# Small e-row moves on ScalarE's queue with two row tiles, and a new order of loads and matrix units between the two passes

## The chip, the cores and the metric

The kernel runs on one core of one Trainium2 chip. Its time is the device time of that core in microseconds (us). Five engines work beside each other: TensorE (PE; its weight loads are listed as PEld), VectorE (DVE), ScalarE (ACT), GpSimd (POOL) and SyncE (SP). SyncE and ScalarE can issue transfers that hardware turns into descriptors, GpSimd issues transfers through software; all of them are carried out by the same 16 DMA engines.

## The reference

One token of width 640 goes through an adaptive-LayerNorm block: attention over a cache (32 heads, 8192 keys, head width 192), then a gated mixer and an MLP (640 to 1536 to 640). The function returns the block's output and the gradients for nine inputs, among them both caches, which are by far the largest tensors (100.7 MB each, and as much again for each gradient).

```
q      = (h @ wq) per head
scores = q . k * Dh**-0.5 ;  p = softmax(scores)
o      = p @ v ;  attn = o @ wo
x1     = x + ga * attn
out    = x1 + gb * B(layernorm(x1) * (1 + cb) + sb)
# gradients wanted: x, k_cache, v_cache, wq, wo, w3, w4, c, w_mod
dV = p^T do          dP = do . V
dS = p * (dP - sum)  dK = dS^T q
```

With a single query, every product of the attention is a matrix with a vector, so the work is reading K once and V twice (once in each pass) and writing dK and dV.

## The kernel before, in words

A head's 8192 keys lie as 128 partitions by 64 rows; a half is 32 rows (1536 KB in bf16), a quarter 16. The work has two passes with a middle between them.

**First pass.** A loop over heads `i` from 0 to 30 holds three heads at once: it computes the scores of head `i`, scales V of head `i - 1` by its exponentials, and finishes head `i - 2`. Scores are a VectorE product (`dot_mul`, L307), a folding sum (L312) and sums of identity matmuls on TensorE (L318). The scaled V tiles (`vs`, four quarters for each head, in a pool of three buffers) feed matmuls with K that build M = K^T (e V) for the head (`m_units`, L391 and L396), which the gradient of q needs later. `m_units` gives four pieces for a quarter, of eight matmuls each: two for the first 128 columns of K and two for the remaining 64. `mp_out` and `m_add` copy M out of PSUM and add its two parts. `E_all` keeps the exponentials of all heads. SyncE issues all loads, in the order in which they stand: K and V halves, wq and w_mod chunks, wo for each pair of heads (`load_wo`, 480 KB, L210), and near the end rows of w4 (L616 to L618).

**Middle.** From L620 head 31 is scored in quarters (`score_mul`, `score_tree`), its exponentials and those of head 30 are multiplied with the unscaled V (`o_rows`, L414), the last pair's output goes through wo (`pair_ao`), and x1 and the two LayerNorms follow as chains of very small VectorE steps with matmuls for the means (`mean_mm`, `mean_sum`). Between them stand the four units `mz[0]` to `mz[3]` of head 29's last quarter, and the row sums `dg_part(n)` (L526), which multiply n of the twelve rows of w4 with a broadcast vector; they use w4 from `w4b`, from `w4x` (a buffer of the `vs` pool) and from `KY` (a K buffer). Then u = LN(x1) @ w3, its gradient and the vectors that the second pass needs (`dao`, `do_r`, `cpr`) are computed.

**Second pass.** It goes over 64 steps `s`, a half of a head each. For each step VectorE multiplies V with `do` (`mul_q`, L1030), TensorE sums (`tree_q`, L1039) to dP, VectorE forms dS (L1334) and dK (`dk_part`, L1055). dV is an outer product: `dv_groups` takes the e rows of the step, which lie across the partitions 0, 32, 64 and 96 in a tile `er_b`, multiplies them with `do` in groups (L1050), and ScalarE copies each group out of PSUM (L1051) into the buffer that GpSimd stores (`store`, L1282). There are eight such groups to a step.

**E rows.** `e_rows(t)` (L337 to L342) transposes the exponentials of a pair of heads on TensorE into PSUM, and ScalarE copies them into a row tile `er_t`. `load_er(s)` (L848 to L854) then moves 32 rows of 256 bytes of it into `er_b[s % 2]`, 8 KB in all, by a DMA from SBUF to SBUF. The first two moves stand just ahead of the second pass (L1013); the later ones are issued in `dv_gen`, where step `s` has done its eighth group: there `load_er(s + 2)` refills the buffer that step `s` has just read. A new row tile is made every fourth step. In between, side jobs (`g_do`, `g_dwo`, `g_chunk` and others) are spread over the steps' slots.

**Order.** From L529 on `tc.manual_schedule(engines=ORDER)` holds for the rest of the kernel: the instructions of TensorE, VectorE, ScalarE and SyncE, with their DMAs, keep the order in which they are written. GpSimd is not in `ORDER`; the framework places its instructions.

```
ORDER = {mybir.EngineType.PE, mybir.EngineType.DVE, mybir.EngineType.Activation, mybir.EngineType.SP}
```

Of the kernel before, what the change touches and what calls it, by code (L numbers as in the profile page):

```python
# [8 lines left out]
FP32 = mybir.dt.float32  # L9
BF16 = mybir.dt.bfloat16  # L10
# [10 lines left out]
def kernel(  # L21
# [26 lines left out]
    nc = tc.nc  # L48
    P = 128
    D = A_x.shape[-1]  # L50
    _, HQ, S, DH = A_k_cache.shape
# [4 lines left out]
    JH = J // 2  # L56
    JQ = J // 4
    TS = 16
    ND = D // P
# [6 lines left out]
    VW = DH + 4  # L66
# [6 lines left out]
    V_, A_, T_ = nc.vector, nc.scalar, nc.tensor  # L73
# [10 lines left out]

    dram = ctx.enter_context(tc.tile_pool(name="dram", bufs=1, space=bass.MemoryType.DRAM))
    ORDER = {mybir.EngineType.PE, mybir.EngineType.DVE, mybir.EngineType.Activation, mybir.EngineType.SP}
    erp = ctx.enter_context(tc.tile_pool(name="erp", bufs=1))

    A_.preload_act_table_set("natural_log_exp_and_others")
    ident_bf = const.tile([P, P], BF16, name="ident_bf")  # L90
# [26 lines left out]
    def mean_mm(src, n):  # L117
        ps = psS.tile([P, 16], FP32, name="mean_ps", tag="s")
        T_.matmul(ps[:, 0:n], lhsT=onesD, rhs=src, start=True, stop=True)
        return ps  # L120
# [86 lines left out]
    def load_wo(t):  # L207

        w = wst.tile([P, 3, D], BF16, name="wo_st", tag="wo")
        nc.sync.dma_start(out=w, in_=wo_v[t])  # L210
        return w
# [41 lines left out]
    n0, r0 = layernorm(x_c, "ln0")  # L253
# [39 lines left out]
    def flat(kb):  # L293
        return kb.rearrange("p j d -> p (j d)")
# [6 lines left out]
    def load_v(h, t, v):  # L301
        nc.sync.dma_start(out=v, in_=V_hd[h][:, t * JH : (t + 1) * JH, :])
        return v
# [24 lines left out]
    H1 = HQ - 1  # L328
    TL = NT - 1
    KX, KY, KC, KD, KE = (KB[(2 * HQ + k) % NKB] for k in (-4, -5, -3, -2, -1))  # L330
# [13 lines left out]
    with tc.tile_pool(name="vs", bufs=3) as vsp, tc.tile_pool(name="ft", bufs=2) as ft, \  # L344
# [40 lines left out]
        def m_units(q, kb, vs, mp, last=3):  # L385
            j0 = (q % 2) * JQ
            z = q == last

            def main(lo, hi):
                for k in range(lo, hi):  # L390
                    T_.matmul(mp[:, 0:MW], lhsT=kb[:, j0 + k, 0:P], rhs=vs[:, k, 0:MW], start=(q == 0 and k == 0), stop=(z and k == JQ - 1), skip_group_check=True)  # L391

            def rest(lo, hi):
                for k in range(lo, hi):
                    p0 = 64 * (k % 2)
                    T_.matmul(mp[p0 : p0 + 64, MO : MO + MW], lhsT=kb[:, j0 + k, P:DH], rhs=vs[:, k, 0:MW], start=False, stop=(z and k >= JQ - 2), skip_group_check=True)  # L396

            return [lambda: main(0, JQ // 2), lambda: main(JQ // 2, JQ), lambda: rest(0, JQ // 2), lambda: rest(JQ // 2, JQ)]
# [11 lines left out]
        def o_rows(h, v2, op, lo, hi):  # L410

            for j in range(lo, hi):
                p0 = 32 * (j % 4)
                T_.matmul(op[p0 : p0 + 32, 0:DH], lhsT=E_all[:, h, j : j + 1].to_broadcast([P, 32]), rhs=v2[j // JH][:, j % JH, :], start=(j < 4), stop=(j >= J - 4), skip_group_check=True)  # L414
# [11 lines left out]
        def mp_out(h, mp):  # L426
            mt = ft.tile([P, MW], FP32, name="mt", bufs=1)
            if h == H1 - 2:
                A_.copy(out=mt[64:128, :], in_=mp[64:128, MO : MO + MW])
            A_.copy(out=M1[:, h, :], in_=mp[:, 0:MW])  # L430
            if h != H1 - 2:
                A_.copy(out=mt[64:128, :], in_=mp[64:128, MO : MO + MW])
            return mt
# [7 lines left out]
        def m_add(h, mp, mt):  # L441
            t, b = divmod(h, 2)
            V_.tensor_tensor(out=M2[64 * b : 64 * b + 64, t, :], in0=mp[0:64, MO : MO + MW], in1=mt[64:128, :], op=ALU.add)
# [28 lines left out]
        X, os_, wo_l = {0: {"k": [load_k(0, 0), load_k(0, 1)], "v": [load_v(0, 0, VB[0])]}}, {}, {}  # L472
# [3 lines left out]
        w4v = B_w4.rearrange("(a p) r -> p a r", p=P)  # L476
# [26 lines left out]
        def w4r(a):  # L503
            if a < 3:
                return w4b[:, a * D : (a + 1) * D]
            if a == 3:
                return w4b[:, 5 * D : 6 * D]
            c0 = (a - 8) * D if a >= 8 else JQ * DH + (a - 4) * D
            return flat(KY)[:, c0 : c0 + D]

        def load_w4(lo, dst, n=4):
            nc.sync.dma_start(out=dst[:, 0 : n * D].rearrange("p (a r) -> p a r", r=D), in_=w4v[:, lo : lo + n, :])

        def w4_at(a):
            if a == 4:
                return w4b[:, 3 * D : 4 * D]
            return w4x[:, (a - 5) * D : (a - 4) * D] if 5 <= a < 8 else w4r(a)

        def dg_junk(a):
            if a == 3:  # L520
                return w4x[:, 3 * D : 4 * D]
            return w4b[:, 3 * D : 4 * D] if a >= 8 else w4_at(a)

        def dg_part(n):
            for a in dgs[:n]:
                V_.tensor_tensor_reduce(out=dg_junk(a), in0=w4_at(a), in1=dbo_bc, scale=1.0, scalar=0.0, op0=ALU.mult, op1=ALU.add, accum_out=d_g[:, a : a + 1])  # L526
            del dgs[:n]

        ctx.enter_context(tc.manual_schedule(engines=ORDER))  # L529
        if True:  # L530
            for i in range(H1):
# [3 lines left out]
                z = X.pop(i - 2) if i > 1 else None  # L535
# [28 lines left out]
                if z is not None:  # L564
                    mt = m_out(i - 2, z["mp"], z["op"], os_)
# [22 lines left out]
                if y is not None:  # L588
                    vs = scale_v(2, y["v"][1], E4, Ef)
# [15 lines left out]
                for f in late:  # L605
                    f()
                nx["v"].append(load_v(i + 1, 0, VB[(2 * i + 2) % NVB]))
                if i % 2 == 1:
                    wo_l[(i + 1) // 2] = load_wo((i + 1) // 2)
                early(i, "end")  # L610
                if i == H1 - 3:

                    w4b = wst.tile([P, ND * CW], BF16, name="w4b", tag="w", bufs=1)
                    dbo_bc, du_bc = w4b[:, 4 * D : 5 * D], w4b[:, 0:F]
                    bcast_cols(dbo, ND, dbo_bc, A_.copy)
                    nc.sync.dma_start(out=w4b[:, 0 : 3 * D].rearrange("p (a r) -> p a r", a=3), in_=w4v[:, 0:3, :])  # L616
                    nc.sync.dma_start(out=w4b[:, 5 * D : 6 * D], in_=w4v[:, 3, :])
                    nc.sync.dma_start(out=w4b[:, 3 * D : 4 * D], in_=w4v[:, 4, :])  # L618
                if i > H1 - 3:
                    dg_part(1)  # L620
            assert mb == NMB and wch is None
# [1 line left out]

            x, y, z = X[H1], X[H1 - 1], X[H1 - 2]
            x["v"].append(load_v(H1, 1, VX))
            mz = m_units(3, z["k"][1], z["vs"], z["mp"])
            x["S"] = ft.tile([P, J], FP32, name="S_h")
            qh = q_at(H1)
# [42 lines left out]
            op_y = psO.tile([P, 256], FP32, name="op")  # L671
            o_rows(H1 - 1, vy, op_y, 0, JH)
            w3d = B_w3.rearrange("(i p) n -> p i n", p=P)
            w4x = vsp.tile([P, JQ, VW], BF16, name="vs").rearrange("p j d -> p (j d)")
            load_w4(5, w4x, 3)
            load_w4(8, flat(KY))
            score_tree(1, d0)
            score_mul(1, 0)
            score_tree(0, d1)
# [6 lines left out]
            w3p = flat(pp.tile([P, JH, DH], BF16, name="w3p", tag="prod"))  # L686
            nc.sync.dma_start(out=w3p[:, 0 : 4 * F].rearrange("p (i n) -> p i n", i=4), in_=w3d[:, 0:4, :])
            nc.sync.dma_start(out=w4b[:, 0:F], in_=w3d[:, 4, :])
            w3v = [w3p[:, k * F : (k + 1) * F] for k in range(4)] + [w4b[:, 0:F]]
            dot_sum(d1, x["S"][:, JH:J])  # L690
            mx = row_max(x["S"])
# [11 lines left out]
            po_x = psr([P, 8], FP32, "po_x")  # L703
            op_x = psO.tile([P, 256], FP32, name="op")
            o_rows(H1, x["v"], op_x, 0, JH)
            o_rows(H1, x["v"], op_x, JH, J)
            es_x = e_sum(H1)
            os_out(1, op_x, es_x)
            dg_part(3)
            for b in range(2):  # L710
                T_.matmul(po_x[64 * b : 64 * b + 64, 3:4], lhsT=onesD[:, 0:64], rhs=os2[:, 2 * DH + b : 2 * DH + b + 1], start=True, stop=True, skip_group_check=True)
            T_.matmul(po_x[:, 4:6], lhsT=onesD, rhs=os2[:, 2 * DH : 2 * DH + 2], start=True, stop=True, skip_group_check=True)
# [8 lines left out]
            V_.tensor_tensor(out=xP, in0=ga, in1=aoP, op=ALU.mult)  # L721
            V_.tensor_tensor(out=xP, in0=xP, in1=x_c, op=ALU.add)
            ps_ao = pair_ao(o2, wo_l[TL], psB, "b")
            mz[1]()
            aoN = col(ND, "aoN")
            V_.reduce_sum(out=aoN, in_=ps_ao, axis=AX.X)
            V_.tensor_tensor(out=x1, in0=ga, in1=aoN, op=ALU.mult)
            V_.tensor_tensor(out=x1, in0=x1, in1=xP, op=ALU.add)
            A_.copy(out=AO[:, :, 2 * TL : 2 * TL + 2], in_=ps_ao)
            ps = mean_mm(x1, ND)  # L730
            mz[2]()
            dg_part(1)
            m = mean_sum(ps, 1, "ln_m")
            xc = col(ND, "ln_xc1")
            V_.tensor_scalar(out=xc, in0=x1, scalar1=m[:, 0:1], scalar2=None, op0=ALU.subtract)
# [1 line left out]
            V_.tensor_tensor(out=pr[:, 0:ND], in0=xc, in1=xc, op=ALU.mult)  # L737
            V_.tensor_tensor(out=pr[:, ND : 2 * ND], in0=xc, in1=a1, op=ALU.mult)
            ps = mean_mm(pr, 2 * ND)
            mz[3]()  # L740
            dg_part(1)
            vt = col(2, "ln_vt")
            V_.reduce_sum(out=vt, in_=ps[:, 0 : 2 * ND].rearrange("p (a b) -> p a b", b=ND), axis=AX.X)
# [7 lines left out]
            ps = mean_mm(pr, 2 * ND)  # L751
            xc2 = col(ND, "ln_xc2")
            V_.scalar_tensor_tensor(out=xc2, in0=zz, scalar=r1[:, 0:1], in1=sS, op0=ALU.mult, op1=ALU.add)
            mt = mp_out(H1 - 2, z["mp"])
            er_t = [e_rows(TL, psB, "b")]
            m_add(H1 - 2, z["mp"], mt)
            ab = mean_sum(ps, 2, "ln_ab")
            v2 = col(1, "ln_v2")
            V_.tensor_scalar(out=v2, in0=ab[:, 0:1], scalar1=r1[:, 0:1], scalar2=ab[:, 1:2], op0=ALU.mult, op1=ALU.add)
# [4 lines left out]
    bst = ctx.enter_context(tc.tile_pool(name="bst", bufs=1))  # L764
# [83 lines left out]
    def load_er(s):  # L848

        er = er_b[s % 2]  # L850
        h, t = ht(s)
        r0 = (h % 2) * J + t * JH
        nc.gpsimd.dma_start(out=er[0:P:32, :, :], in_=er_t[0][r0 : r0 + JH, :])  # L853
        return er  # L854

    def ht(s):
# [149 lines left out]
    nc.sync.dma_start(out=dao_bc, in_=dao_d.to_broadcast([P, D]))  # L1006
    V_.tensor_scalar(out=dx1, in0=e4, scalar1=vv[:, 0:1], scalar2=-1.0, op0=ALU.add, op1=ALU.mult)
    V_.tensor_tensor(out=dao, in0=dx1, in1=ga, op=ALU.mult)
    cpp, cp1 = bst.tile([P, DH], FP32, name="dq_junk")[:, 0 : HQ * ND].rearrange("p (h k) -> p h k", k=ND), bst.tile([P, HQ], FP32, name="cp1")
    V_.tensor_tensor(out=cpp, in0=AO.rearrange("p k h -> p h k"), in1=dao[:, None, :].to_broadcast([P, HQ, ND]), op=ALU.mult)  # L1010
    V_.reduce_sum(out=cp1, in_=cpp, axis=AX.X)
    V_.memset(er_b[1], 0.0)
# [400 lines left out]
```

## Time and profile before

| | |
|---|---|
| median of 4 runs | 1409.81 us (1403.95 to 1410.89) |
| the profiled execution: its own time | 1403.95 us |
| its span, first to last instruction | 1402.2 us |
| mean granted TensorE clock | 0.793 |
| DMA: bytes, mean rate | 570.88 MB, 407 GB/s |
| busy: PE / DVE / ACT / POOL | 80% / 79% / 63% / 11% |

The profile is one execution of the program. In groups and in the timeline a line gives the start or the count, the busy time in us, the engine, the line of the kernel, the operation and its tiles as out<-in; `[1.13 <-DMA KB]` at its end says that the engine stood idle for 1.13 us before it and what ended that. SPq and ACTq are the DMA issues of those engines, shown apart from their work. The time to landing of a DMA runs from its issue until its completion is seen. Lines of stages (A:B in us) give each engine's busy time and count, then the granted clock as a share, the DMA engines' mean busy share and the rate in GB/s.

### The profile page before, as it was taken

The page shows a single profiled execution, that of the slowest core. Times are in us where ns is not written, and L with a number is a line of the kernel's source. Part 1 is how long each engine was busy: PE and PEld are TensorE (multiplying, and loading weights), DVE is VectorE, ACT ScalarE, POOL GpSimd, SP SyncE. Part 2 cuts the span into 40 slices and gives each one's busy share as a digit, 9 for nine tenths or more (in the row PEclk, how much of TensorE's full clock was granted, in tenths as well). Part 3 has the DMA queues.
Part 4 walks back from the last instruction along what each step waited for, and adds up shares of the span by engine and source line. Part 5 has one row for each costly group of instructions (what it writes and reads, how often), then busy time and mean ns, then how long its engine had stood idle before and what let it go on. Part 6 is the DMA issues. An engine that isn't in the chain of part 4 may idle for free. (4 is left out here: it accounts for less than half of the span.)

```text
span 1402.2 us, 30000 instructions
## 1 busy us (share of the span) xinstructions
PE 1121.0 (80%) x12543; PEld 741.2 (53%) x12543; DVE 1108.7 (79%) x1380; ACT 877.8 (63%) x1934; POOL 152.6 (11%) x270
## 2 busy tenths in 40 slices
PE   3899999899999998777767777777776877866773
PEld 1677777677767767444444444444443444433441
DVE  4999999999999998785767667776676766866783
ACT  0777777777777773655656565565565665655663
POOL 0000000000000001311111111111111111211111
PEclk9999999999999998766775666566685555677765
DMA  9999999999999998899999999999999999999998
GB/s 375 409 420 419 420 416 413 414 404 416 422 417 420 414 417 322 315 364 425 424 420 421 412 423 425 421 415 416 424 420 423 409 413 413 405 421 423 390 402 344
DMA packets 82264, 570.88 MB, mean 407 GB/s; under 512 B 12464, under 2 KB 31232, under 8 KB 42192
## 3 DMA queue, kind: packets, MB, share of 16 engines
q1 hardware_dynamic: 55372, 342.48, 60.1%
q0 software_dynamic: 26736, 226.48, 38.9%
q8 instruction: 98, 1.61, 0.4%
q14 instruction: 38, 0.31, 0.1%
q10 hardware_dynamic: 20, 0.00, 0.0%
HBM read 341.64 MB, written 225.91 MB: 405 GB/s over the span
## 5 line engine op out<-in xcount | busy, mean ns | idle before, releaser
L1051 ACT CAST KB<-dv_ps 128x768 bf16<-128x768 f32 x416 | 315.2, 804 | 203.5 <-PE dv_ps L1050 195.5
L1039 PE MATMUL dot_ps<-w3p,ident_bf 128*128 128x256 bf16 x1536 | 328.3, 376 | 87.9 <-DVE w3p L1030 87.3
L376 ACT ACTIVATE vs<-VB,Ef 128x192 bf16<-128x192 bf16 x840 | 303.2, 443 | 0.0
L1039 PEld LDWEIGHTS <-ident_bf 128*128 128x128 bf16 x1536 | 176.9, 125 | 196.8 <-issue 145.3
L1050 PE MATMUL dv_ps<-do_r,er_b 32*128 32x192 bf16 x2048 | 202.5, 305 | 64.9 <-ACT KB L1051 44.5
L307 DVE TENSOR_TENSOR prod<-KB,q_ring 128x6144 bf16<-128x6144 bf16 x62 | 207.9, 3353 | 15.9 <-DMA KB<-in_A_k_cache_dram 11.7
L1055 DVE TENSOR_TENSOR KB<-q_ring,dS 128x3072 bf16<-128x3072 bf16 x100 | 175.2, 1753 | 46.0 <-DMA out_dram<-KB 32.1
L391 PE MATMUL mp<-vs,KB 128*128 128x193 bf16 x1920 | 182.1, 246 | 0.0
L1050 PEld LDWEIGHTS <-er_b 32*128 32x128 bf16 x2048 | 84.6, 105 | 174.6 <-issue 161.2
L391 PEld LDWEIGHTS <-KB 128*128 128x128 bf16 x1920 | 162.5, 97 | 17.6 <-issue 5.5
L1030 DVE TENSOR_TENSOR w3p<-VB,do_r 128x3072 bf16<-128x3072 bf16 x96 | 168.1, 1751 | 0.0
L318 PE MATMUL dot_ps<-prod,ident_bf 128*128 128x512 bf16 x372 | 94.0, 390 | 47.2 <-DVE prod L312 47.0
L322 DVE TENSOR_REDUCE dP<-dot_ps 128x32 f32<-128x512 f32 x64 | 44.2, 690 | 105.3 <-PE dot_ps L1039 105.3
L369 DVE TENSOR_TENSOR vs<-VB,E 128x1728 bf16<-128x1728 bf16 x120 | 123.6, 1051 | 0.0
L312 DVE TENSOR_TENSOR prod<-prod 128x3072 bf16<-128x3072 bf16 x62 | 108.7, 1754 | 1.0
L1051 ACT CAST VX<-dv_ps 128x768 bf16<-128x768 f32 x96 | 73.1, 806 | 53.8 <-PE dv_ps L1050 50.4
L874 ACT COPY wT<-wT_ps 128x1024 bf16<-128x1024 bf16 x84 | 81.0, 964 | 37.1 <-PE wT_ps L873 36.8
L396 PE MATMUL mp<-vs,KB 128*64 128x193 bf16 x1920 | 103.8, 251 | 0.0
L853 POOL DMA_DIRECT2D er_b<-er_t x64 | 40.4, 631 | 568.1 <-PE dv_ps L1050 271.8
L396 PEld LDWEIGHTS <-KB 128*64 128x64 bf16 x1920 | 77.3, 110 | 19.2 <-issue 19.1
L356 ACT ACTIVATE E<-S_h,negm 128x256 bf16<-128x256 f32 x30 | 15.2, 508 | 109.5 <-DVE negm L553 109.5
L318 PEld LDWEIGHTS <-ident_bf 128*128 128x128 bf16 x372 | 37.6, 105 | 85.0 <-issue 56.7
(350 smaller groups left out, 1150.8 us busy)
## 6 DMA issues: line engine op xcount, KB each, us to landing
VB<-in_A_v_cache_dram SPq DMA_DIRECT2D x108, 1536.0 KB, 12.2
out_dram<-KB POOLq DMA_DIRECT2D x100, 1536.0 KB, 17.1
KB<-in_A_k_cache_dram SPq DMA_DIRECT2D x63, 1536.0 KB, 11.8
out_dram<-VX POOLq DMA_DIRECT2D x25, 1536.0 KB, 17.1
KB<-in_A_v_cache_dram SPq DMA_DIRECT2D x15, 1536.0 KB, 12.9
wo_st<-in_A_wo_dram SPq DMA_DIRECT2D x30, 480.0 KB, 11.9
w_st<-in_A_wq_dram SPq DMA_DIRECT2D x12, 960.0 KB, 12.2
out_dram<-wo_st POOLq DMA_DIRECT2D x16, 480.0 KB, 18.8
```

The source lines that it names most:

```text
L307: V_.tensor_tensor(out=prod, in0=src, in1=vec[:, None, :].to_broadcast([P, JH, DH]), op=ALU.mult)
L312: V_.tensor_tensor(out=prod[:, :, 0:w], in0=prod[:, :, 0:w], in1=prod[:, :, w : 2 * w], op=ALU.add)
L318: T_.matmul(ps, lhsT=ident_bf, rhs=prod[:, :, k : k + TS], start=(k == 0), stop=(k == w - TS))
L369: V_.tensor_tensor(out=vs[:, 0:n, 0:DH].rearrange("p j (a b) -> p j a b", b=4), in0=v[:, v0 : v0 + n, :].rearrange("p j (a b) -> p j a b", ...
L376: A_.activation(out=vs[:, k, 0:DH], in_=v[:, v0 + k, :], func=ACT.Copy, scale=Ef[:, j0 + k : j0 + k + 1])
L391: T_.matmul(mp[:, 0:MW], lhsT=kb[:, j0 + k, 0:P], rhs=vs[:, k, 0:MW], start=(q == 0 and k == 0), stop=(z and k == JQ - 1), skip_group_chec ...
L396: T_.matmul(mp[p0 : p0 + 64, MO : MO + MW], lhsT=kb[:, j0 + k, P:DH], rhs=vs[:, k, 0:MW], start=False, stop=(z and k >= JQ - 2), skip_grou ...
L1030: V_.tensor_tensor(out=pq[:, q], in0=v_l[s][:, q * JQ : (q + 1) * JQ, :], in1=do_of(ht(s)[0])[:, None, :].to_broadcast([P, JQ, DH]), op=AL ...
L1039: T_.matmul(ps[:, q * JQ : (q + 1) * JQ, :], lhsT=ident_bf, rhs=pq[:, q, :, k : k + TS], start=(k == 0), stop=(k == DH - TS), skip_group_c ...
L1050: T_.matmul(ps[:, b, k * DH : (k + 1) * DH], lhsT=er[p0 : p0 + 32, 2 * m + k, :], rhs=doh[p0 : p0 + 32, :], start=True, stop=True)
L1051: A_.copy(out=dV4[:, 2 * q : 2 * q + 2, m * PW : (m + 1) * PW], in_=ps[:, :, 0:PW])
L1055: V_.tensor_tensor(out=dK[:, lo:hi, :].rearrange("p j (a b) -> p j a b", b=4), in0=qh.rearrange("p (a b) -> p a b", b=4)[:, None, :, :].to ...
```

## The change

Three groups of edits are made at once.

- `load_er` issues its DMA on ScalarE's queue instead of GpSimd's. The pool of row tiles has two buffers instead of one. To make room, `cp1` becomes a part of the tile `dq_junk` instead of a tile of its own.
- The order of loads ahead of the middle: wo of the last pair and row 4 of w4 are no longer issued in the loop. Behind the load of head 31's second V half come rows 4 to 7 of w4 into `w4x` (rows 5 to 7 before), then wo of the last pair. Rows 8 to 11 of w4 into `KY` are issued behind the two loads of w3.
- The order of instructions in the middle: `mz[1]` and `mz[2]` go between the two halves of head 31's `o_rows`, `mz[3]` goes to where `mz[1]` was, `mp_out` and `m_add` go from the second LayerNorm to the place of x1's mean, and the row sums are grouped as 4, 1 and 1 in place of 3, 1, 1 and 1.

```diff
-    erp = ctx.enter_context(tc.tile_pool(name="erp", bufs=1))
+    erp = ctx.enter_context(tc.tile_pool(name="erp", bufs=2))
...
         def w4_at(a):
-            if a == 4:
-                return w4b[:, 3 * D : 4 * D]
-            return w4x[:, (a - 5) * D : (a - 4) * D] if 5 <= a < 8 else w4r(a)
+            return w4x[:, (a - 4) * D : (a - 3) * D] if 4 <= a < 8 else w4r(a)
 
         def dg_junk(a):
-            if a == 3:
-                return w4x[:, 3 * D : 4 * D]
-            return w4b[:, 3 * D : 4 * D] if a >= 8 else w4_at(a)
+            return w4b[:, 3 * D : 4 * D] if a == 3 or a >= 8 else w4_at(a)
...
-                if i % 2 == 1:
+                if i % 2 == 1 and i + 1 < H1 - 1:
                     wo_l[(i + 1) // 2] = load_wo((i + 1) // 2)
...
                     nc.sync.dma_start(out=w4b[:, 5 * D : 6 * D], in_=w4v[:, 3, :])
-                    nc.sync.dma_start(out=w4b[:, 3 * D : 4 * D], in_=w4v[:, 4, :])
...
             x["v"].append(load_v(H1, 1, VX))
+            w4x = vsp.tile([P, JQ, VW], BF16, name="vs").rearrange("p j d -> p (j d)")
+            load_w4(4, w4x)
+            wo_l[TL] = load_wo(TL)
...
-            w4x = vsp.tile([P, JQ, VW], BF16, name="vs").rearrange("p j d -> p (j d)")
-            load_w4(5, w4x, 3)
-            load_w4(8, flat(KY))
             score_tree(1, d0)
...
             nc.sync.dma_start(out=w4b[:, 0:F], in_=w3d[:, 4, :])
+            load_w4(8, flat(KY))
...
             o_rows(H1, x["v"], op_x, 0, JH)
+            mz[1]()
+            mz[2]()
             o_rows(H1, x["v"], op_x, JH, J)
             es_x = e_sum(H1)
             os_out(1, op_x, es_x)
-            dg_part(3)
+            dg_part(4)
...
             ps_ao = pair_ao(o2, wo_l[TL], psB, "b")
-            mz[1]()
+            mz[3]()
...
             A_.copy(out=AO[:, :, 2 * TL : 2 * TL + 2], in_=ps_ao)
+            mt = mp_out(H1 - 2, z["mp"])
             ps = mean_mm(x1, ND)
-            mz[2]()
-            dg_part(1)
+            m_add(H1 - 2, z["mp"], mt)
             m = mean_sum(ps, 1, "ln_m")
...
             ps = mean_mm(pr, 2 * ND)
-            mz[3]()
             dg_part(1)
...
-            mt = mp_out(H1 - 2, z["mp"])
             er_t = [e_rows(TL, psB, "b")]
-            m_add(H1 - 2, z["mp"], mt)
             ab = mean_sum(ps, 2, "ln_ab")
...
-        nc.gpsimd.dma_start(out=er[0:P:32, :, :], in_=er_t[0][r0 : r0 + JH, :])
+        A_.dma_start(out=er[0:P:32, :, :], in_=er_t[0][r0 : r0 + JH, :])
...
-    cpp, cp1 = bst.tile([P, DH], FP32, name="dq_junk")[:, 0 : HQ * ND].rearrange("p (h k) -> p h k", k=ND), bst.tile([P, HQ], FP32, name="cp1")
+    cpj = bst.tile([P, DH], FP32, name="dq_junk")
+    cpp, cp1 = cpj[:, 0 : HQ * ND].rearrange("p (h k) -> p h k", k=ND), cpj[:, HQ * ND : HQ * (ND + 1)]
```

## The prediction

> **What bounds the kernel now.** I read the page's forty slices first, then stages of the span by busy time, then the tile that the change moves (er_b), then the order of instructions around the middle.
>
> ```profile
> DMA  9999999999999998899999999999999999999998
> GB/s 375 409 420 419 420 416 413 414 404 416 422 417 420 414 417 322 315 364 425 424 420 421 412 423 425 421 415 416 424 420 423 409 413 413 405 421 423 390 402 344
> ...
> 0.00:553.00 553.00, 490.69 (x7176) 375.69 (x7176) 517.30 (x533) 375.70 (x1193) 10.00 (x29) 1.00 1.00 410
> 553.00:620.00 67.00, 52.59 (x670) 36.12 (x670) 53.00 (x112) 39.67 (x73) 19.13 (x32) 0.72 0.89 309
> 620.00:1300.00 680.00, 514.92 (x4160) 294.40 (x4157) 472.35 (x667) 406.48 (x592) 107.06 (x182) 0.65 1.01 419
> 1300.00:1402.00 102.00, 62.82 (x543) 35.02 (x541) 66.07 (x70) 55.97 (x79) 16.37 (x28) 0.68 0.93 378
> ```
>
> The stage lines give PE, weight loads, VectorE, ScalarE, GpSimd busy us, then the clock, the DMA share and GB/s. Before 553 and from 620 to 1300 the DMA engines are full (share 1.00 and 1.01). There a shorter wait on a compute engine changes only how early a transfer queues. Time is lost where DMA is starved: 553 to 620 moves 309 GB/s instead of 419, which is 67 x (1 - 309/419) = 17.6 us, and the tail loses 102 x (1 - 378/419) = 10.0 us. What moves the start of the second pass moves the end.
>
> ```profile
> L853 POOL DMA_DIRECT2D er_b<-er_t x64: 619/629/647, 554.3 to 1368.6; - x64
> ...
>   PEld L1050: 9.1, 6
>   PE dv_ps L1050: 7.6, 4
>   ACT er_t L341: 4.1, 1
> ...
> DMA to landing us min/median/max: 3.9/9.4/17.4
> ```
>
> An e-row move takes GpSimd 0.63 us to issue and lands 3.9 to 17.4 us later; TensorE waited for it four times (7.6 us), ScalarE once (4.1 us).
>
> ```profile
> 535.44 3.63 DVE L632 TENSOR_TENSOR pb<-KB,q_ring 128x3072 bf16<-128x3072 bf16 x2 [1.13 <-DMA KB<-in_A_k_cache_dram]
> 544.67 0.84 PE L414 MATMUL op<-VX,E_all 128*32 128x192 bf16 x32 [0.93 <-DMA VX<-in_A_v_cache_dram]
> 546.00 0.82 DVE L526 CUSTOM_DVE_ANT_0 vs<-vs,w4b 128x640 bf16<-128x640 bf16 x1 [1.39 <-DMA vs<-in_B_w_dram]
> 552.68 0.35 DVE L443 TENSOR_TENSOR M<-mp,mt 64x193 f32<-64x193 f32 x1 [0.50 <-ACT M L430]
> 554.34 0.65 POOL L853 DMA_DIRECT2D er_b<-er_t  x1 [0.29 <-POOL er_b L776]
> 567.14 0.82 PE L1050 MATMUL dv_ps<-do_r,er_b 32*128 32x192 bf16 x8
> 567.25 0.16 ACT L1004 COPY h<-h_ps 128x5 f32<-128x5 f32 x1 [0.61 <-PE h_ps L907]
> 574.70 0.69 DVE L322 TENSOR_REDUCE dP<-dot_ps 128x32 f32<-128x512 f32 x1 [1.51 <-PE dot_ps L1039]
> ```
>
> The middle waits on three loads (K, VX, w4x), 0.9 to 1.4 us each. The e rows of step 0 were issued at 554.34, 12.8 us ahead of their reader at 567.14: GpSimd's order is not among the written ones, so this move ran ahead of its place in the text.
>
> **The change, part by part.**
>
> *Loads.* wo of the last pair (480 KB) and row 4 of w4 (160 KB) leave the sync queue ahead of head 31's second K half and V. 655,360 bytes at 420 GB/s is 1.56 us: K and VX land up to that much earlier. On K only 1.13 us can be used, since VectorE is busy until 534.31. VX would land at 543.1 instead of 544.67. Behind VX now come w4 rows 4 to 7 (640 KB instead of rows 5 to 7), then wo, at about 545.8, ahead of its reader at 547.87. The load of w4 rows 8 to 11 goes behind the two w3 loads, so it no longer issues at 531.12 but after the product buffer is free (540.62). The bytes until then are the same, so it lands when the last w3 row did, 541.09 + 11.5 = 552.6, ahead of its reader at 553.77. That cover is 1.2 us; past it each microsecond late delays u by one. The price lies between 0 and 1.5; I take 0.
>
> *M units.* Two of eight matmuls (0.85 us each, 1.7) now stand between the halves of head 31's o rows. E of head 31 comes 1.1 us earlier, the first half ends at about 542.6, the units at 544.3, and the second half starts there, 0.3 us earlier than before instead of 1.5. Where they stood (548.24, 549.62, 551.08) they cost about 0.1 us each at the next matmul. So nearly all of VX's gain goes into them.
>
> *Row sums on VectorE.* Four rows in place of three come before the reciprocal of head 31's sum. Row 4 now needs w4x (about 544.65), and three rows from there at 0.8 us end at 547.1; the reciprocal stood at 547.17. What is left of the 0.3 us is gone. If w4x is 0.7 us later, x1 is 0.7 later. The row taken out behind x1 (548.90) had filled a wait for the mean: nothing.
>
> *Last M addition.* It leaves the place where it cost 0.4 us (mean ready near 552.65, sum at 553.07) and goes between x1's mean and its sum: ScalarE's two copies (0.32 each) follow the unit that ends at 549.08, the addition ends near 550.2, the sum moves from 549.73 to there: +0.5. Together +0.1.
>
> For the middle I bound the sum by -1.1 (all of the K wait) and +1.2 (addition and w4x late), and take 0.1.
>
> *First e-row move.* ScalarE's order is a written one. The move stands behind the copy of h, which ends at 567.41, so it issues there and no longer at 554.34. The issue costs ScalarE 0.27 to 0.56 us by the only two DMAs that ScalarE issues (at the start of the span). Those landed at 4.6 with the second issue done at 1.61, 3.0 us. A small store on the sync queue near 566.7 released its reader's issue at 569.0, 2.3 us. The slowest near row is GpSimd's quiet minimum, 3.9 us. So it lands at 569.7 to 571.4. I take 570.3, by the two hardware-issued rows, where TensorE had begun at 567.14: +3.2 us, bounds 2.6 and 4.2. Behind this wait on TensorE stand the sum for cpr, all step-0 score trees and all step-0 dV groups; VectorE's dP (574.70) had already waited 1.51 us for the trees, so the delay passes whole to dP, the product of step 1, the V loads of step 4 on and the stores. DMA share was 0.76 from 567 to 580, nothing is queued to fill the gap, and I pass 3.2 on. If something hides it the price is 0.
>
> *The other 63 moves.* They go straight behind ScalarE's copy of the eighth dV group, which has already waited for the matmuls that free the buffer: no new semaphore wait of length. ScalarE spends 63 x 0.3 = 19 us more in 830; it was busy 406.5 of 680 us, so about 5.1 us of each 12.8 us step is free. (57 moves between 638.84 and 1368.6 give 12.8.) Hidden; I take 0.2 for the last steps. GpSimd gives back 40 us that nobody waits for: the store behind each move waits for the same dV group's 0.8 us copy anyway.
>
> The longest row against this: the second of two sync-queue issues side by side takes 1.1 to 1.5 us instead of 0.33 (w3's second load, 1.47), and the longest single issue 4.46. The Trainium skill (Perfetto Trace Analysis, DMA Instruction - HWDGE) says that the descriptor generator is locked for exclusive use by one sequencer, and that the profiled window includes that wait. By that rule a ScalarE move that meets a sync load stands still with every copy behind it; at 1.5 us each on all 63 it would hold ScalarE for 95 us, still within the free 5.1 us a step, so the sum by the rule is the same.
>
> *Waits that go.* TensorE's and ScalarE's waits on er_b from 620 to 1300 (3.0, 2.0, 2.3 and ScalarE's 4.07 at 1085) vanish: a quick move, and two row tiles. But DMA is full there. Dips follow only two of them: 398 GB/s in 910 to 920 and 393 and 400 in 1090 to 1110, against 421: 0.5 + 0.7 + 0.5 = 1.7 us. I take -1.7; bounds 0 and -9.6, the whole gap from 419 to the better slices' 425 over 680 us.
>
> *No cost:* cp1 as a part of dq_junk: it is read at 567.90 and next written over at 577.74, and both shift alike. The other scrap target of the row sums changes no instruction.
>
> **Sum** against the profiled execution's own 1403.95 us (span 1402.2 and 1.75 around it): 0.1 + 3.2 + 0.2 - 1.7 = +1.8, 1405.75. The median of the runs shown is 5.86 above that execution, so the forecast is 1409.81 + 1.8 = 1411.6.
>
> **Rivals.** *First move hidden* (its delay meets slack at 593, where VectorE waited 3.56 us for a store): 0.1 + 0.2 - 1.7 = -1.4, 1408.4. For it: that wait. Against: the store itself is issued by the chain that is late.
>
> *ScalarE held at its issues* (the slower side). TensorE has two dV buffers and waits for ScalarE's copies 48 us from 640 to 1340. It is busy 514.9 of 680, 9.7 us a step, so it can lose 3.1 us. Once a move holds ScalarE longer, each step grows: at the longest sync issue, 4.46, by 1.4 us, 57 steps 78 us. It decides from 3.2 us a move on (57 x 0.1 plus the 1.8 is over 7). Against it: sync loads issue behind VectorE's product, some 2 us ahead of the move. I place it at 1417 to 1440.
>
> *The e rows starved the second pass* (faster). If the late moves cause all of the 9.6 us between 419 and 425 GB/s: 0.1 + 3.2 + 0.2 - 9.6 = -6.1, 1403.7; with the K gain, -7.3, 1402.5. For it: moves that took 13.8 us ahead of the wait at 626. Against: most dips have no er_b wait near them.
>
> **How the numbers follow.** Forecast 0.55 (1407 to 1416), hidden 0.16, held 0.17, starved 0.12, of which 0.10 falls beyond 0.5% (7.0 us, about what a measurement of this kernel can tell from no change: the four runs span 6.9). From the forecast 0.01 is over 1416.9. So faster 0.10, same 0.72, slower 0.18. The range 1402.5 to 1420 leaves out about 0.08 below and 0.10 above.
>
> **What the changed profile would show.** The first er_b move on ScalarE's queue near 567.5, and TensorE's first dV matmul idle some 3 us behind it; VX's wait gone and the units at 543; the VectorE sum after x1 waiting for the copies of M; moves landing in 2 to 4 us with no er_b wait behind 620; 620 to 1300 still at share 1.0 and about 420 GB/s. I am wrong if the first move issues well before 567, if ScalarE's issues take over 3 us, or if the DMA share from 620 on falls.

## The result and the profile after

The changed kernel's median is 1415.27 us (1409.86 to 1420.82, 32 runs), the kernel before's 1409.68 us (1403.23 to 1418.69, 53 runs beside them). The ratio is 1.0038, 95% interval [1.0027, 1.0049]: 5.4 us slower, less than the 0.5% that the prediction set as its bound, but clear of zero. The forecast was +1.8 us; 3.6 us were not foreseen. The profiled executions take 1403.95 us before, which is one of its fastest, and 1416.04 us after, which is near its median. So a difference between the two traces has some 6 us of scatter in it, and where the text below says what an edit costs, it goes by the times of several runs.

The forty slices of the changed kernel, DMA share and rate, and its stages (columns as in the prediction):

```profile
DMA  9999999999999998799999999999999999999988
GB/s 376 404 420 419 418 417 409 416 401 418 421 418 419 414 411 318 287 361 427 426 426 425 408 424 423 418 410 414 412 409 421 425 403 416 408 412 423 372 347 351
...
553.00:620.00 67.00, 50.03 (x635) 34.13 (x635) 49.07 (x112) 36.34 (x67) 15.54 (x30) 0.69 0.81 283
620.00:1300.00 680.00, 507.90 (x4156) 291.67 (x4155) 472.82 (x665) 404.81 (x588) 74.16 (x130) 0.66 1.01 417
1300.00:1402.00 102.00, 74.81 (x584) 41.01 (x582) 70.68 (x76) 62.02 (x88) 11.60 (x21) 0.63 0.91 364
```

From 620 to 1300 the DMA engines are as full as before (share 1.01, 417 against 419 GB/s). The loss sits at both ends of the second pass: 553 to 620 falls from 309 to 283 GB/s, 1300 to 1402 from 378 to 364. At 419 GB/s the first is 67 x 26 / 419 = 4.2 us of transfers that come later, the second 102 x 14 / 419 = 3.4 us.

The start of the second pass in the timeline of the changed kernel:

```profile
568.23 0.16 ACT L999 COPY h<-h_ps 128x5 f32<-128x5 f32 x1 [0.61 <-PE h_ps L902]
568.29 1.31 ACTq L848 DMA_DIRECT2D er_b<-er_t  x2
571.86 0.82 PE L1046 MATMUL dv_ps<-do_r,er_b 32*128 32x192 bf16 x8 [3.66 <-DMA er_b<-er_t]
579.40 0.69 DVE L322 TENSOR_REDUCE dP<-dot_ps 128x32 f32<-128x512 f32 x1 [3.91 <-PE dot_ps L1035]
```

The first move issues behind the copy of h, as forecast, and TensorE then stands idle for 3.66 us until the e rows land. VectorE's first dP is 4.7 us later than before (574.70). Of that 0.98 us is the copy of h itself, which was at 567.25; 0.77 of the 0.98 was there at 528 already, where both programs still do the same work.

What the changed kernel's trace says of the tile er_b, and its middle:

```profile
L848 ACTq DMA_DIRECT2D er_b<-er_t x64: 542/543/654, 568.3 to 1384.9; - x64
...
  PEld L1046: 5.9, 3
  PE dv_ps L1046: 5.4, 3
```

```profile
528.90 1.05 DVE L369 TENSOR_TENSOR vs<-VB,E 128x1728 bf16<-128x1728 bf16 x1
533.33 3.42 DVE L630 TENSOR_TENSOR pb<-KB,q_ring 128x3072 bf16<-128x3072 bf16 x2
543.32 0.85 PE L391 MATMUL mp<-vs,KB 128*128 128x193 bf16 x8
544.10 0.52 PE L396 MATMUL mp<-vs,KB 128*64 128x193 bf16 x8
544.55 0.84 PE L414 MATMUL op<-VX,E_all 128*32 128x192 bf16 x32
545.48 0.83 DVE L522 CUSTOM_DVE_ANT_0 vs<-vs,w4b 128x640 bf16<-128x640 bf16 x1 [1.97 <-DMA vs<-in_B_w_dram]
550.13 0.35 DVE L443 TENSOR_TENSOR M<-mp,mt 64x193 f32<-64x193 f32 x1 [0.61 <-ACT M L430]
550.51 0.16 DVE L124 TENSOR_REDUCE ln_m<-mean_ps 128x1 f32<-128x5 f32 x1
```

In the kernel before, the same product near 528 and the sum of x1's mean stood at

```profile
528.13 1.05 DVE L369 TENSOR_TENSOR vs<-VB,E 128x1728 bf16<-128x1728 bf16 x1
549.73 0.16 DVE L124 TENSOR_REDUCE ln_m<-mean_ps 128x1 f32<-128x5 f32 x1
```

TensorE's waits on er_b fall from 7.6 us to 5.4, 3.66 of it the first one. In the middle the waits for K and VX are gone, the wait for w4x stays (1.97 us), and head 31's second half of o rows starts at 544.55 where it started at 544.67. Counted from 528, where this trace is 0.77 us late already, that is 0.9 us earlier; the prediction had 0.3, since it gave the two M units 1.7 us between the halves and they take 1.23 (543.32 to 544.55). The wait for w4x and the M addition use up the gain: x1's mean is summed 0.78 us later than before, which is the same 0.77 again.

**What the prediction did not look for** is on GpSimd, whose instructions the framework places. With the e-row moves gone from its queue, it placed the stores anew. Before, dV's store goes out ahead of dK's of the same step in all 60 steps from step 4 on; after, dK's goes first in 48 of them. The store of dV is not issued later for that: in both traces it goes out 0.3 us (median) after its last copy. What moves is dK's, from 3.8 us after its product to 0.3. Two w_mod chunk stores (960 KB each) that the source holds back until the last steps were issued at 1360.88 and 1370.60 before, and at 1310.34 and 1346.28 after. Output buffers turn in a ring of five, and step s's dK is written into the buffer of dV of step s - 2 (number 2s + 1 takes that of 2s - 4). So the store that VectorE waits for next is dV's. GpSimd's stores and VectorE's products into VX near 1310 to 1335, before:

```profile
1308.43 0.55 POOL L1282 DMA_DIRECT2D out_dram<-VX  x1 [0.21 <-issue]
1308.97 0.53 POOL L1282 DMA_DIRECT2D out_dram<-KB  x1
1320.48 1.75 DVE L1055 TENSOR_TENSOR VX<-q_ring,dS 128x3072 bf16<-128x3072 bf16 x1
```

and after:

```profile
1310.34 0.88 POOL L1130 DMA_DIRECT2D out_dram<-stg  x1 [9.05 <-DVE stg L1126]
1313.68 0.55 POOL L1278 DMA_DIRECT2D out_dram<-KB  x1 [2.46 <-DVE v_bf L1102]
1316.43 0.53 POOL L1278 DMA_DIRECT2D out_dram<-VX  x1 [2.20 <-ACT VX L1047]
1333.39 1.76 DVE L1051 TENSOR_TENSOR VX<-q_ring,dS 128x3072 bf16<-128x3072 bf16 x1 [4.79 <-DMA out_dram<-VX]
```

Before, VX was written again 12.05 us after its store was issued, with no wait. After, dK's 1536 KB (and a w_mod chunk) stand ahead of VX's store in GpSimd's queue; the buffer came free 17.0 us after the issue, and VectorE waited 4.79 us. Over steps 4 to 63 the median time from issue to landing goes from 13.7 to 15.2 us for dV's stores and from 19.0 to 13.8 for dK's.

### The profile page after: what moved, and what is told of

It reads as the page before. It is cut to its first block, busy times and chain, and to the rows that moved or that the text cites. A ratio compares the mean times of both kernels' runs of the same rounds, so it can differ in the third digit from the quotient of the medians.

```text
span 1414.3 us, 29988 instructions
## 1 busy us (share of the span) xinstructions
PE 1124.0 (79%) x12543; PEld 742.9 (53%) x12543; DVE 1109.9 (78%) x1380; ACT 878.8 (62%) x1934; POOL 112.1 (8%) x206
## 4 chain that ended last, share of the span: by engine, by line
issue 37%; DVE 24%; DMA 18%; PE 13%; POOL 5%; ACT 2%; POOLq 0%; SPq 0%; DVEq 0%; ACTq 0%
DVE prod L307 9%; DMA KB<-in_A_k_cache_dram 7%; DVE prod L312 5%; DMA out_dram<-KB 5%; POOL out_dram L1278 3%; DVE vs L369 3%; PE mp L391 3%; PE dot_ps L1035 3%; DMA out_dram<-VX 3%; PE dot_ps L318 2%; PE mp L396 2%; DVE S_h L322 2%; DVE w3p L1026 1%; DMA VB<-in_A_v_cache_dram 1%; DMA vs<-in_B_w_dram 1%
## 5 line engine op out<-in xcount | busy, mean ns | idle before, releaser
L1278 POOL DMA_DIRECT2D out_dram<-KB x104 | 56.2, 541 | 491.4 <-DVE KB L1051 224.5
L356 ACT ACTIVATE E<-S_h,negm 128x256 bf16<-128x256 f32 x30 | 15.2, 508 | 107.9 <-DVE negm L549 107.9
```

## The experiments

Four theories, each with a price that a time can show. M: the middle. F: the late first e-row move. R: the other 62 moves, with what they change elsewhere. Within R, the order of GpSimd's stores, which splits into dK ahead of dV and the early w_mod chunks. The expectations of the first runs put these theories partly in other words or with other names; the price beside each tells which is meant. Each run below is told by its ratio to the kernel before, measured beside it, and by its mean over all runs with one standard error; differences between two experiments are of these means, with twice the error of the difference as interval. The kernel before ran beside each group of them, with means from 1409.6 to 1410.3 us.

**1. The first two moves on GpSimd** (the changed kernel; the rest stays on ScalarE).

```diff
-        A_.dma_start(out=er[0:P:32, :, :], in_=er_t[0][r0 : r0 + JH, :])
+        (A_ if s >= 2 else nc.gpsimd).dma_start(out=er[0:P:32, :, :], in_=er_t[0][r0 : r0 + JH, :])
```

> The changed kernel, but the first two e-row moves are issued by GpSimd as before. Theory 1 (the late first move is the cost): the first dV matmul no longer waits, starts near 568, and the time is 3 to 4 us under the changed kernel, about +1.5 us on the kernel before. Theory 2 (without the e-row moves on its queue GpSimd's stores are placed in another order, dK of a step ahead of its dV, and the stores are late): the changed kernel's time stays, +4 to +6 us on the kernel before, although the first wait is gone.

Measured: 1.0007 [0.998, 1.0034], mean 1411.56 +- 0.83. That is 3.7 us [1.7, 5.6] below the changed kernel: F is real, and about as large as TensorE's wait.

**2. Only the first two moves on ScalarE** (kernel before).

```diff
-        nc.gpsimd.dma_start(out=er[0:P:32, :, :], in_=er_t[0][r0 : r0 + JH, :])
+        (A_ if s < 2 else nc.gpsimd).dma_start(out=er[0:P:32, :, :], in_=er_t[0][r0 : r0 + JH, :])
```

> The kernel before, with only the first two e-row moves on ScalarE's queue; all others, the store order of the second pass and the middle as before. Theory 1: first dV matmul some 3.5 us later, +3 to +4 us in time. Theory 2: the delay is taken up by slack in the second pass, 0 to +1 us.

Measured: 1.0017 [0.9993, 1.004], mean 1412.13 +- 1.10, 2.4 us above before. In its trace TensorE waits 3.49 us for the first rows. The sign agrees with F, the interval takes in zero, so alone it decides nothing.

**3. Only the middle** (kernel before with the change's load and middle edits; the moves stay on GpSimd with one row tile). The edits at their core:

```diff
             x["v"].append(load_v(H1, 1, VX))
+            w4x = vsp.tile([P, JQ, VW], BF16, name="vs").rearrange("p j d -> p (j d)")
+            load_w4(4, w4x)
+            wo_l[TL] = load_wo(TL)
...
             o_rows(H1, x["v"], op_x, 0, JH)
+            mz[1]()
+            mz[2]()
             o_rows(H1, x["v"], op_x, JH, J)
...
-            dg_part(3)
+            dg_part(4)
```

> The kernel before with only the edits of the loads and of the middle; all e-row moves on GpSimd, one row tile. Theories 1 and 2: within 1 us of the kernel before (VX's gain is spent on the matrix units). A third theory, that the middle's new order itself costs the time: +3 us or more, with the first dV matmul later by as much.

Measured: 1.0002 [0.9981, 1.0022], mean 1409.97 +- 0.83: M is nothing, within 3 us either way.

**4. Only the moves from step 2 on** (kernel before, two row tiles with the room made as in the change, first two moves on GpSimd).

```diff
-    erp = ctx.enter_context(tc.tile_pool(name="erp", bufs=1))
+    erp = ctx.enter_context(tc.tile_pool(name="erp", bufs=2))
...
-        nc.gpsimd.dma_start(out=er[0:P:32, :, :], in_=er_t[0][r0 : r0 + JH, :])
+        (A_ if s >= 2 else nc.gpsimd).dma_start(out=er[0:P:32, :, :], in_=er_t[0][r0 : r0 + JH, :])
```

> The kernel before with e-row moves 2 to 63 on ScalarE's queue, two row tiles and cp1 in dq_junk; the first two moves and the middle as before. Theory 1: no loss, 0 to -2 us (the waits for er_b behind 620 us vanish). Theory 2: +2 to +5 us, with GpSimd waiting for dK before it stores a dV that is ready.

Measured: 1.0014 [0.9993, 1.0034], mean 1411.90 +- 0.72. TensorE's er_b waits are down to 0.6 us, and yet the time is 2.2 us up, not 1.5 down. In this trace, too, GpSimd's stores are in the new order (dK first in the same 48 of 60 steps; in experiments 2 and 3, whose later moves stay on GpSimd, in none), and VectorE waits 6.0 us for VX's store. This pointed to the order of the stores.

**5. GpSimd's stores back in the written order** (changed kernel).

```diff
-    ORDER = {mybir.EngineType.PE, mybir.EngineType.DVE, mybir.EngineType.Activation, mybir.EngineType.SP}
+    ORDER = {mybir.EngineType.PE, mybir.EngineType.DVE, mybir.EngineType.Activation, mybir.EngineType.SP, mybir.EngineType.Pool}
```

> The changed kernel with GpSimd added to the engines whose order is the written one, so that its stores stand as in the kernel before: dV of a step ahead of its dK, and the two held-back w_mod chunks (960 KB each) at the steps third and second from the end. Theory 3 (the change cost twice: the first move comes late, and the planner moved the two held-back stores out of the tail): 2 to 4 us under the changed kernel, about +3 on the kernel before, and the stretch from the dP of step 56 to the end back from about 99 to about 96 us. Theory 1 (only the first move): no gain on the changed kernel, +5.

Measured: 1.0023 [0.9998, 1.0048], mean 1413.28 +- 1.25: 2.0 us [-0.7, 4.6] below the changed kernel. The sign is that of the theory, the size not yet clear of zero. The stretch from the dP of step 56 to the end is back from 99.2 to 96.4 us, as expected, but it is no measure of the loss: experiment 8 has 105.1 us there at the time of the kernel before.

**6. The written order, and the first move early** (experiment 5, and `load_er(0)` issued on ScalarE straight behind the second group of w3 transposes, some 13 us ahead of its reader).

```diff
     w3t_pe(2)
+    er_0 = load_er(0)
...
-    er_l = {0: load_er(0), 1: load_er(1)}
+    er_l = {0: er_0, 1: load_er(1)}
```

> The kernel of the run above with the first e-row move written on ScalarE's queue where the row tile and er_b are ready (behind the first two w3 transposes), and not behind the copy of h. Theory 3: both costs are gone, 0 plus or minus 1.5 us on the kernel before. Theory 1 predicts the same of the first move alone, so that this kernel and the one above differ by 3 to 4 us. If something else in the change costs time, +3 or more stays.

Measured: 1.0002 [0.9981, 1.0023], mean 1408.89 +- 1.14: both losses gone. The start of its second pass in the timeline:

```profile
553.45 0.64 ACTq L789 DMA_DIRECT2D er_b<-er_t  x1
566.30 0.82 PE L1047 MATMUL dv_ps<-do_r,er_b 32*128 32x192 bf16 x8
566.41 0.16 ACT L1000 COPY h<-h_ps 128x5 f32<-128x5 f32 x1 [0.61 <-PE h_ps L903]
```

TensorE starts just ahead of the copy of h with no wait, as in the kernel before: what costs is the move's place, not the queue that issues it.

**7. The first move later still** (changed kernel with twelve more ScalarE copies ahead of it, whose results nothing uses).

```diff
+    for _ in range(12):
+        A_.copy(out=v_bc, in_=dbo_bc[:, 0:PW])
     er_l = {0: load_er(0), 1: load_er(1)}
```

> The changed kernel with twelve copies of 128x384 on ScalarE ahead of the first two moves (about 0.5 us each, 6 us; their result is not used). If the late first move passes whole to the end, as the prediction had it: +5 to +7 us on the changed kernel, +10 to +12 on the kernel before. If slack takes up the delay: under +2 on the changed kernel, and the first move's 3.7 us would not explain it.

Measured: 1.0064 [1.004, 1.0088], mean 1418.40 +- 0.74 over 7 runs, 3.2 us [1.4, 5.0] above the changed kernel. The start of its second pass:

```profile
567.24 6.49 ACT L1010 COPY v_bc<-w4b 128x384 bf16<-128x384 bf16 x12
573.28 1.23 ACTq L848 DMA_DIRECT2D er_b<-er_t  x2
575.16 0.82 PE L1048 MATMUL dv_ps<-do_r,er_b 32*128 32x192 bf16 x8 [8.02 <-DMA er_b<-er_t]
```

Both traces do the same work up to 528, where this one is 0.98 us ahead of the changed kernel's. Counted from there, the move issues 6.0 us later, but its reader starts only 4.3 us later (575.16 - 571.86 + 0.98), since this move took 1.9 us from issue to reader where the other took 3.6. At the end 3.2 us [1.4, 5.0] of it are seen. That is less than the +5 to +7 that was expected, which took the whole 6 us to reach the reader, and more than the +2 of slack: most of the delay passes to the end, and all of it may.

**8. The w_mod chunks not held** (kernel before, both stores issued when their chunk is ready).

```diff
             keep = lambda w=cur["w"]: nc.gpsimd.dma_start(out=dst[:, :, lo : lo + CW], in_=w)
-            if dst is dwm_v and n in (GX - 2, GX - 1):
-                kept.append(keep)
-            else:
-                keep()
+            keep()
...
-        if s in (NS - 4, NS - 3):
-            kept.pop(0)()
```

> The kernel before, whose two held-back w_mod stores go out as soon as their chunk is done; nothing of the change in it. Theory 3: +2 to +4 us on the kernel before, with a tail that looks like the changed kernel's (last dV group some 14 us ahead of the end, not 20). If the held-back stores don't matter: within 1 us.

Measured: 1.0001 [0.998, 1.0022], mean 1409.99 +- 0.99. The end of its trace looks like the changed kernel's (VectorE idle 5.36 us at VX), but the time is that of before. So the early chunks are not the loss, and neither is one such wait in itself. A reason that fits, but is not shown: while the DMA engines are still full, a chunk that goes out early is one that need not go out at the end.

**9. The first move early, GpSimd left to the framework** (experiment 6 without its edit of `ORDER`).

```diff
-    ORDER = {mybir.EngineType.PE, mybir.EngineType.DVE, mybir.EngineType.Activation, mybir.EngineType.SP, mybir.EngineType.Pool}
+    ORDER = {mybir.EngineType.PE, mybir.EngineType.DVE, mybir.EngineType.Activation, mybir.EngineType.SP}
```

> The changed kernel with one edit: the first e-row move stands on ScalarE's queue straight behind the second group of w3 transposes, as in the run that also wrote GpSimd's order out; GpSimd's order is left to the planner. With the changed kernel, the run with GpSimd's order and the run with both this makes a square of two edits. Theory F with R (late first move about 4 us, GpSimd's other store order about 2 us, adding up): the first dV matmul near 568, the held w_mod stores early again (near 1305 and 1342), ratio to the kernel before about 1.0014, 1411.5 us. Rival (the late first move is all of the loss, the store order nothing): ratio 1.000, the time of the kernel before within 1 us. Rival (the two parts hide each other, what is saved at the first move is lost in the tail): ratio 1.003 or more, as the changed kernel.

Measured: 1.0012 [0.9991, 1.0033], mean 1411.69 +- 0.77, 3.5 us [1.7, 5.4] below the changed kernel. With the changed kernel and experiments 5 and 6 it makes a square: late and placed 1.0038, late and written 1.0023, early and placed 1.0012, early and written 1.0002. The two edits add up within the noise: by the means the written order saves 2.0 us with the late move and 2.8 with the early one, a difference of 0.8 +- 1.9.

**10. Written order, early first move, chunks not held** (experiment 6 with the edit of experiment 8).

```diff
-            if dst is dwm_v and n in (GX - 2, GX - 1):
-                kept.append(keep)
-            else:
-                keep()
+            keep()
...
-        if s in (NS - 4, NS - 3):
-            kept.pop(0)()
```

> The run with GpSimd's written order and the early first move, with one edit: the two held w_mod stores (960 KB each) are issued when their chunk is ready and not four and three steps from the end. Theory R by the held stores: the last steps lengthen (step 56 to 63 near 79 us instead of 70.8, the end after step 63 about 20 instead of 24) and the time is about 2 us above that run, ratio 1.0015 to the kernel before. Rival (where these two stores stand is nothing, since the DMA engines move the same bytes until the end): the two stretches change in the same way, their sum stays, ratio 1.000 within 0.001.

Measured: 0.9991 [0.9972, 1.001], mean 1407.05 +- 0.70. The held stores are out again, now in this base, with no loss. It is the fastest version tried, and by its ratio not clear of the kernel before.

**11. dK's store ahead of dV's, written by hand** (experiment 6). From step 4 on, the dK store that now goes first is that of the same step, in all 60 steps (the expectation says half for the framework's order; it is 48 of 60).

```diff
-                    store(dV_hd, s, dV, JQ if s == 0 else 0, JH)
+                    put = lambda s=s, dV=dV: store(dV_hd, s, dV, JQ if s == 0 else 0, JH)
+                    if s > 0:
+                        later.append(put)
+                    else:
+                        put()
...
         store(dK_hd, s, dK, JQ if s < 2 else 0, JH)
+        while later:
+            later.pop(0)()
```

> The run with GpSimd's written order and the early first move, with one edit: from step 1 on the dV store of a step is issued behind the dK store of the step before it and not ahead of it, as the planner did in some half of the changed kernel's steps. The held w_mod stores stay late. Theory (the order of dV and dK is the loss of R): about 2.4 us above that run, ratio 1.0015 to 1.002, and VectorE waits 3 us or more for a store of an output buffer between 1300 and 1400, where that run has 1.3. Rival (the order of the two is nothing, since the same bytes are in the queue): ratio 1.000 within 0.001.

Measured: 1.0015 [0.9999, 1.0032], mean 1412.02 +- 0.61: 3.1 us [0.5, 5.7] above experiment 6. Its VX store and the product that waits for it:

```profile
1312.27 0.53 POOL L1279 DMA_DIRECT2D out_dram<-KB  x1 [12.03 <-DVE v_bf L1103]
1315.18 0.53 POOL L1279 DMA_DIRECT2D out_dram<-VX  x1 [2.38 <-ACT VX L1048]
1329.22 1.76 DVE L1052 TENSOR_TENSOR VX<-q_ring,dS 128x3072 bf16<-128x3072 bf16 x1 [3.12 <-DMA out_dram<-VX]
```

The w_mod chunks are late here, and the wait is there all the same. VectorE's waits for stores of output buffers from 620 to 1300 (engine, line, tile, what it waited for: us, times, longest) in this experiment and in experiment 6:

```profile
DVE KB L1052 <- DMA out_dram<-KB: 56.4, 17, 6.7
DVE VX L1052 <- DMA out_dram<-VX: 10.2, 4, 4.6
```

```profile
DVE KB L1052 <- DMA out_dram<-KB: 7.0, 3, 4.2
DVE VX L1052 <- DMA out_dram<-VX: 5.1, 2, 4.4
```

**12. Both by hand** (experiment 11 with the edit of experiment 8).

```diff
-            if dst is dwm_v and n in (GX - 2, GX - 1):
-                kept.append(keep)
-            else:
-                keep()
+            keep()
...
-        if s in (NS - 4, NS - 3):
-            kept.pop(0)()
```

> The same edit, and the two held w_mod stores issued when their chunk is ready: the two differences that the traces show between the planner's order and the written one, made by hand. Theory (R is the planner's order): near the run with the early first move alone, ratio 1.0012, 1411 to 1412 us, a VectorE wait of 4 to 6 us for VX's store near 1330. Rival (neither order costs; the differences of 2 us between the runs are noise): ratio 0.999 to 1.000, as in the runs with the written order.

Measured: 1.0023 [1.0009, 1.0038], mean 1413.39 +- 0.81, slower than before beyond doubt, and 6.4 us [4.2, 8.5] above experiment 10, which has the same edits but for the order of dV and dK.

Put side by side, five kernels with an early first move on ScalarE differ in the order of the stores:

| first move early; stores | mean us | VectorE's waits for output stores, 620 to 1300 | the same, from 1300 |
|---|---|---|---|
| 6: dV first, chunks held | 1408.89 | 12.1 | 1.3 |
| 10: dV first, chunks early | 1407.05 | 9.0 | 0 (3.05 with no releaser shown) |
| 9: placed by the framework (dK first in 48 of 60 steps, chunks early) | 1411.69 | 60.7 | 5.3 |
| 11: dK first, chunks held | 1412.02 | 66.6 | 5.1 |
| 12: dK first, chunks early | 1413.39 | 69.0 | 5.1 |

The three with dK first (36 runs, 1412.37 +- 0.43) are 4.4 us [2.8, 6.0] above the two with dV first (24 runs, 1407.97 +- 0.68). By the ratios, each to the kernel before beside it, the same difference is 1.0017 - 0.9997, or 2.8 us [0.4, 5.2]. Experiments 9 and 10, which ran beside the same runs of the kernel before, are 4.6 us [2.6, 6.7] apart by their means and 3.0 by their ratios. So that the order costs time is shown; the size is some 3 to 4 us. Experiments 1 and 4, which have the early first move and the placed order too, agree with 9: they are 1.9, 2.2 and 2.0 us above before.

That it does so through VectorE's waits for the buffers is argued from the traces and not shown: most of these waits fall where the DMA engines are full (share 1.01), the kernel before has 40.1 us of them with dV first, experiment 3 has 53.3 at no loss, and experiment 8 has a long one at the end without a loss. Which of the waits make up the loss is open.

## Why the prediction was right and wrong

**The class, the sign and the range held; the size did not.** The forecast of +1.8 us lies below the measured interval of +3.8 to +6.9 (0.27% and 0.49% of 1410). The range of 1402.5 to 1420 was wide enough to hold a result from which a whole term of the sum was missing; that it held does not make the sum right.

**The middle, 0.1 within -1.1 to +1.2:** right as far as can be told. The K and VX waits went, the w4x wait stayed, and experiment 3 measured +0.3 +- 1.1. The parts were less exact than their sum: the M units took 1.23 us and not 1.7, and the mean's sum, counted from 528, came where it was before and not 0.5 us later. By the copy of h the middle is 0.2 us longer in these two traces.

**The first move, 3.2 within 2.6 to 4.2:** right mechanism, undersized by half a microsecond. TensorE's wait is 3.66 us, since the issue takes 0.54 us (two issues, 1.31) and the landing 3.0 behind it. Three comparisons by time give 3.5, 3.7 and 4.4 us (9, 1, and 5 against 6), and experiment 7 agrees that such a delay passes to the end, if not exactly how much of it. The rival "first move hidden" is out.

**The other moves, 0.2:** the issue is 0.543 us, not 0.3, so 64 moves take 35 us of ScalarE and not 19. They are still hidden; experiments 6 and 10 hold all of them at no loss. The rival "ScalarE held at its issues" is out: the longest issue is 654 ns. The Trainium skill (Perfetto Trace Analysis, DMA Instruction - HWDGE) says that the descriptor generator is locked for one sequencer at a time; no issue of ScalarE here shows a wait for it beyond the 0.1 us between median and maximum.

**The step that failed** is this sentence of the prediction: "GpSimd gives back 40 us that nobody waits for: the store behind each move waits for the same dV group's 0.8 us copy anyway." It treated the stores as fixed behind the move. They are not: GpSimd isn't in `ORDER`, and with the moves gone the framework put dK's store, ready some 3 us earlier, ahead of dV's, whose buffer is the one wanted next. All five kernels whose later moves left GpSimd with its order placed (the changed one, 1, 4, 7 and 9) have dK first in the same 48 of 60 steps, and those whose later moves stay there (before, 2, 3 and 8) in none; by what rule the framework chooses is not shown. By the means this costs 2.0 us [-0.7, 4.6] with the late first move (changed kernel against 5) and 4.4 [2.8, 6.0] with the early one, 2.8 by the ratios. The prediction had used the same freedom for the first move ("ran ahead of its place in the text") and had not asked what else it moves.

**The waits that go, -1.7 within 0 to -9.6:** they did go, 7.6 us to 1.7 behind the first. No gain can be seen in the changed kernel, whose rate from 620 to 1300 is 417 GB/s. Where the order of the stores is kept and the first move is early, experiments 6 and 10 are 0.7 and 2.6 us below before (weighted -1.8 +- 0.85 by the means, -0.6 +- 1.0 by the ratios), so the -1.7 may be there; neither alone is clear of zero by its ratio. No run has the written order of GpSimd with the moves left on it, so what the two gained cannot be put down to the er_b waits alone. The rival "the e rows starved the second pass", -6 us, is out.

In sum, as an estimate from these means: 0.3 for the middle, 3.7 for the first move, 2.0 to 4.4 for the order, and -1.8 for the rest give 4.2 to 6.6; the measured difference is 5.4.

## What to carry to other kernels

Before an instruction is taken off an engine whose order is left to the framework, ask what that order will be without it: here a move that cost GpSimd 0.63 us had kept dV's store ahead of dK's, and losing it cost some 2 to 4 us of 1410, at least as much as the moves' own waits could give back. A move that is put on an engine with a written order issues where it is written, so write it as early as its data allow; 13 us ahead of its reader it was free, and behind the last copy it cost its whole 3.7 us. In a queue of stores, try the one whose buffer is written next first, even if another is ready sooner; here that was worth some 3 to 4 us.

## What the runs showed of the hardware

- A DMA of 8 KB within SBUF holds ScalarE's queue for 0.54 us and was there for its reader 1.9 us after the issue at best (experiment 7), 3.4 to 3.6 us in the changed kernel and in experiments 2 and 5. Issued by GpSimd it took 3.9 to 17.4 us in the kernel before.
- With the DMA engines full (share 1.01), a store's landing hangs on what was issued ahead of it on the same queue. Over steps 4 to 63 the median time from issue to landing was 13.6 us for dV's stores and 19.0 for dK's where dV's goes first (experiment 6), and 15.0 and 12.7 where dK's does (experiment 11). VX's 1536 KB were free again within 12.05 us in the kernel before, with dK's store behind it, and after 17.0 us in the changed kernel, with dK's store and a chunk ahead. The Trainium skill (DMA: Bandwidth & Descriptors, Two DMAs through the same engine are not ordered) says that within one queue of one DMA engine descriptors start in order; these times fit it.
